# q and k transposed by DMA, the norm in four-head chunks, rsqrt by Ln and Exp: attention into a sine-gated MLP on one core

## The chip, the cores and the metric

One core of one Trainium2 chip runs the whole program. The metric is device time of one execution in microseconds (us); the kernel before has a median of 743.25 us over three runs (742.65 to 746.86).

## What is computed

Eight batches of 12 heads, 448 tokens, head size 64. q and k are normalised over the head (root mean square, with gains), then softmax attention, then an MLP over all 3584 tokens. Cut to what matters:

```python
def rmsnorm(x, g):
    rms = np.sqrt(np.mean(x * x, axis=-1, keepdims=True) + 1e-06)
    return x / rms * g
q_n, k_n = rmsnorm(q, g_q), rmsnorm(k, g_k)
attn = softmax(q_n @ k_n.T / sqrt(64))          # per batch and head
x = (attn @ v), heads side by side: 3584 x 768
h = x @ w_in                                    # 768 x 2048
g = h + sin(alpha * h)**2 / (alpha + 1e-09)
out = g @ w_out                                 # 2048 x 768
```

## The kernel before, in words

The order of the work is written out by hand; each engine takes its instructions in the order of the program, and waits where an operand is late.

**Per batch** there is an attention phase of six head pairs (index `p`), and then a first product and a second product. For a pair, `scores` (L225) makes four blocks of transposed scores on TensorE (PE) from `qkT`, ScalarE (ACT) takes the exponentials, and `attend` (L242), one pair later, multiplies by v and by a matrix of ones, which gives the row sums. ACT makes the reciprocal as Exp(-Ln(sum)) (L260, L261), and VectorE (DVE) writes the scaled result to `xT` (L264). After six pairs `first_product` (L282) runs 16 column tiles, with Sin and Square on ACT and GpSimd (POOL), and a final operation on DVE (L278). The second product of a batch (`second_product`, L312) is cut into steps of two matmuls, which are filled in between the scores of the next batch: 48 steps after an even batch, 64 after an odd one. The last batch's stand at the end.

**The norm.** q and k are loaded (L92, L98, on SP's queue) with the tokens on the partitions, in groups of six heads (`gi`, two groups per batch). `norm_tasks` (L146) gives a list of small tasks: squares on POOL (L158), sums over 64 on DVE (L161), the product of the two gains folded into k on POOL (L165), mean plus epsilon on DVE (L168), the power -0.5 on POOL for both q and k at once (L172, `inv`), and six scalings on DVE to bf16 (L178). `bg(n)` runs the next n tasks between the pieces of a pair and in the first product. At pair 2 and at the end of the batch what is left is run at once.

**The transposes.** Two pairs ahead, `transposes` (L210) turns a pair's q and k on PE into PSUM (L218, L221), and DVE copies them to `qkT` (L223). It takes one of the four PSUM bank pairs, which are handed out in a ring to scores, attend, transposes and both products.

**v** is loaded on POOL's queue, with a cast to bf16: five DMAs for each group (L92, L98). w_in comes in one DMA on POOL's queue before the first scores, w_out in one at the first pair.

Of the kernel before, what the change touches and what calls it, by code (L numbers as in the profile page):

```python
# [31 lines left out]
def kernel(  # L32
# [56 lines left out]
    def load_group(src, dst, gi, eng):  # L89
        b, h0 = gi // 2, (gi % 2) * GH  # L90
        for t in range(NT):
            eng.dma_start(  # L92
                out=dst[:, t * GH:(t + 1) * GH, :],
                in_=src[b, h0:h0 + GH, t * P:(t + 1) * P, :].rearrange("h p d -> p h d"),
            )
        rest = src[b, h0:h0 + GH, NT * P:S, :].rearrange("(pr two) p d -> two p pr d", two=2)
        for hi in range(2):
            eng.dma_start(out=dst[hi * 64:(hi + 1) * 64, NT * GH:SLOTS, :], in_=rest[hi])  # L98

    qf, kf, vb, qn, kn = {}, {}, {}, {}, {}  # L100

    def load_qk(gi):
        qf[gi] = inp.tile([P, SLOTS, D], F32, tag="qf", name="qf")
        kf[gi] = inp.tile([P, SLOTS, D], F32, tag="kf", name="kf")
        load_group(q, qf[gi], gi, nc.sync)
        load_group(k, kf[gi], gi, nc.sync)

    def load_v(gi):
        vb[gi] = vpool.tile([P, SLOTS, D], BF16, tag="vb", name="vb")
        load_group(v, vb[gi], gi, nc.gpsimd)  # L110
# [32 lines left out]
    NCH = 3  # L143
    CH = SLOTS // NCH

    def norm_tasks(gi):  # L146
# [3 lines left out]
        def begin():  # L150
            st["ms"] = npool.tile([P, 2, SLOTS], F32, tag="ms", name="ms")
            qn[gi] = npool.tile([P, SLOTS, D], BF16, tag="qn", name="qn")
            kn[gi] = npool.tile([P, SLOTS, D], BF16, tag="kn", name="kn")

        def square(which, c):
            src = (qf, kf)[which][gi]
            st[which, c] = sqpool.tile([P, CH, D], F32, tag="sq", name="sq")
            nc.gpsimd.tensor_mul(st[which, c], src[:, c * CH:(c + 1) * CH, :], src[:, c * CH:(c + 1) * CH, :])  # L158

        def reduce(which, c):  # L160
            nc.vector.reduce_sum(st["ms"][:, which, c * CH:(c + 1) * CH], st[which, c], axis=AX.X)  # L161

        def fold_g(c):
            sl = kf[gi][:, c * CH:(c + 1) * CH, :]
            nc.gpsimd.tensor_mul(sl, sl, gg.to_broadcast([P, CH, D]))  # L165

        def mean():
            nc.vector.tensor_scalar(st["ms"], st["ms"], 1.0 / D, 1e-6, op0=ALU.mult, op1=ALU.add)  # L168
# [6 lines left out]
        def scale(which, c):  # L175
            src, dst = (qf, kf)[which][gi], (qn, kn)[which][gi]
            lo = which * SLOTS + c * CH
            nc.vector.tensor_mul(  # L178
                dst[:, c * CH:(c + 1) * CH, :], src[:, c * CH:(c + 1) * CH, :],
                st["inv"][:, lo:lo + CH].unsqueeze(2).to_broadcast([P, CH, D]))  # L180

        work = [begin]
        pend = None
        for which in range(2):
            for c in range(NCH):
                work.append(lambda w=which, c=c: square(w, c))
                if pend:
                    work.append(pend)
                pend = lambda w=which, c=c: reduce(w, c)
        work.append(lambda: fold_g(0))  # L190
        work += [pend, mean, rsqrt, lambda: fold_g(1), lambda: fold_g(2)]
        for which in range(2):
            for c in range(NCH):
                work.append(lambda w=which, c=c: scale(w, c))
        return work
# [7 lines left out]
    qkT, expT, xT = {}, {}, {}  # L203

    def token_columns(b):


        return (REST, 0) if b % 2 else (0, NT * P)

    def transposes(pi):  # L210

        gi, pl = pi // GP, pi % GP
        tp = psum.tile([P, 2, 1024], BF16, tag="ps", name="tp")
# [216 lines left out]
```

## Time and profile before

| what | us |
|---|---|
| median of three runs | 743.25 |
| the profiled execution: its own time | 741.66 |
| its span | 739.9 |
| busy: PE, DVE, ACT, POOL | 542.2, 322.8, 333.8, 385.9 |

The profile is of one execution, with a span from the first to the last instruction. Durations are read from that execution, so a sum of changes stands against 741.66 us; the median is 1.6 us more. Busy shares are means over phases with different limits: PE is busy for 73% of the span, and yet there are stretches in which it waits. The TensorE clock that was granted has a mean of 0.908 of full speed.

### The profile page before, as it was taken

How to read it: one execution, taken by the hardware profiler on the slowest of the kernel's cores; microseconds unless marked ns; L12 is line 12 of the kernel's file. 1: busy time of each engine (PE TensorE's matmuls, PEld its weight loads, DVE VectorE, ACT ScalarE, POOL GpSimd, SP SyncE). 2: the span in 40 equal slices, each digit the busy share in tenths (PEclk: the TensorE clock that was granted, in tenths of full speed). 3: DMA queues.
4: the chain of work that ended last, by engine and by line, in shares of the span. 5: the costliest groups of instructions: out<-in, count | busy, mean ns of one | idle time of the engine just before them, and what ended most of it. 6: DMA issues, size and time to landing. Idle time of an engine off the chain costs nothing.

```text
span 739.9 us, 8666 instructions
## 1 busy us (share of the span) xinstructions
PE 542.2 (73%) x3296; PEld 237.9 (32%) x3296; DVE 322.8 (44%) x464; ACT 333.8 (45%) x496; POOL 385.9 (52%) x312
## 2 busy tenths in 40 slices
PE   0316567949689497859779497885779778799787
PEld 0102223414334143323234243332334323344344
DVE  2345743454434654454534635347434355321331
ACT  0114435625465245634455335652546334566530
POOL 5997943496254853587243962566625674200210
PEclk9976879979999799988899789996989978999999
DMA  9999600540423413360420704243313430000002
GB/s 160 152 199 198 83 1 0 81 54 22 97 20 79 58 51 68 40 94 23 96 18 24 114 22 97 20 97 40 67 30 41 97 41 21 1 23 22 22 16 70
DMA packets 142201, 45.46 MB, mean 61 GB/s; under 512 B 135760, under 2 KB 137808, under 8 KB 142160
## 3 DMA queue, kind: packets, MB, share of 16 engines
q1 hardware_dynamic: 95024, 33.12, 19.9%
q0 software_dynamic: 47136, 11.80, 16.2%
q8 instruction: 25, 0.41, 0.2%
q14 instruction: 16, 0.13, 0.1%
HBM read 45.69 MB, written 11.01 MB: 77 GB/s over the span
## 4 chain that ended last, share of the span: by engine, by line
PE 40%; ACT 15%; POOL 15%; DVE 14%; issue 8%; SPq 5%; DMA 2%; DVEq 0%; ACTq 0%; POOLq 0%
PE ops L324 13%; PE hps L289 13%; POOL inv L172 12%; ACT s L270 10%; PE av L258 7%; DVE kn L178 5%; ACT s L275 4%; DVE qn L178 4%; SPq L92 3%; PE sc L234 2%; POOL sq L158 2%; PE tp L218 2%; SPq L98 2%; DMA kf<-in_k_dram 1%; DVE qkT L223 1%
## 5 line engine op out<-in xcount | busy, mean ns | idle before, releaser
L289 PE MATMUL hps<-xT,w_in_sb 128*128 128x448 bf16 x768 | 171.7, 373 | 65.9 <-ACT s L270 56.2
L238 ACT ACTIVATE expT<-sc 128x896 bf16<-128x896 f32 x144 | 125.7, 914 | 186.9 <-PE sc L234 186.8
L324 PE MATMUL ops<-w_out_sb,g_sb 128*128 128x384 bf16 x896 | 177.2, 331 | 0.0
L273 POOL TENSOR_TENSOR s<-s 128x448 f32<-128x448 f32 x64 | 59.6, 932 | 210.1 <-ACT s L270 188.2
L172 POOL TENSOR_TENSOR inv<-ms,mhalf 128x42 f32<-128x42 f32 x16 | 113.4, 7087 | 63.2 <-DVE ms L168 62.9
L278 DVE SCALAR_TENSOR_TENSOR g_sb<-s,inv_alpha_sb,hps 128x448 bf16<-128x448 f32 x128 | 81.4, 677 | 133.6 <-ACT s L270 133.6
L270 ACT ACTIVATE s<-hps,alpha_sb 128x448 f32<-128x448 f32 x128 | 80.3, 627 | 113.0 <-PE hps L289 111.5
L289 PEld LDWEIGHTS <-w_in_sb 128*128 128x128 bf16 x768 | 77.4, 102 | 158.3 <-issue 102.0
L324 PEld LDWEIGHTS <-g_sb 128*128 128x128 bf16 x896 | 74.5, 98 | 66.1 <-issue 28.3
L178 DVE TENSOR_TENSOR qn<-qf,inv 128x448 bf16<-128x448 f32 x48 | 57.6, 1251 | 85.1 <-POOL inv L172 85.1
L264 DVE TENSOR_TENSOR xT<-av,rec 128x448 bf16<-128x448 f32 x48 | 29.7, 619 | 105.1 <-ACT rec L261 105.1
L234 PE MATMUL sc<-qkT 64*128 64x448 bf16 x288 | 48.3, 389 | 34.8 <-DVE xT L264 27.4
L218 PE MATMUL tp<-ident,qn 128*128 128x128 bf16 x144 | 17.5, 232 | 76.1 <-DVE qn L178 43.2
L158 POOL TENSOR_TENSOR sq<-kf 128x448 f32<-128x448 f32 x48 | 43.7, 928 | 52.5 <-DVE ms L161 52.5
L258 PE MATMUL av<-expT,vb 128*64 128x448 bf16 (+1 forms) x384 | 57.3, 399 | 3.8 <-ACT expT L238 3.3
L165 POOL TENSOR_TENSOR kf<-kf,gg 128x448 f32<-128x448 f32 x48 | 59.6, 1252 | 0.0
L161 DVE TENSOR_REDUCE ms<-sq 128x7 f32<-128x448 f32 x96 | 55.1, 609 | 6.9 <-POOL sq L158 6.8
L258 PE MATMUL av<-expT,ones 128*64 128x448 bf16 (+1 forms) x384 | 54.6, 384 | 0.0
L260 ACT ACTIVATE rec<-av 128x448 f32<-128x448 f32 x48 | 26.1, 543 | 61.9 <-PE av L258 61.9
L223 DVE COPY qkT<-tp 128x896 bf16<-128x896 bf16 x48 | 29.8, 620 | 44.8 <-PE tp L221 44.7
L158 POOL TENSOR_TENSOR sq<-qf 128x448 f32<-128x448 f32 x48 | 47.8, 1037 | 0.4 <-DMA qf<-in_q_dram 0.4
L178 DVE TENSOR_TENSOR kn<-kf,inv 128x448 bf16<-128x448 f32 x48 | 47.8, 1035 | 0.0
(33 smaller groups left out, 350.9 us busy)
## 6 DMA issues: line engine op xcount, KB each, us to landing
qf<-in_q_dram SPq DMA_DIRECT2D x48, 192.0 KB, 3.9
kf<-in_k_dram SPq DMA_DIRECT2D x48, 192.0 KB, 3.8
out_dram<-osb SPq DMA_DIRECT2D x24, 384.0 KB, 2.3
vb<-in_v_dram POOLq DMA_DIRECT2D x48, 96.0 KB, 3.4
w_in_sb<-in_moe_w_in_dram POOLq DMA_DIRECT2D x1, 3072.0 KB, 20.8
w_out_sb<-in_moe_w_out_dram POOLq DMA_DIRECT2D x1, 3072.0 KB, 22.9
qf<-in_q_dram SPq DMA_DIRECT2D x32, 48.0 KB, 3.5
kf<-in_k_dram SPq DMA_DIRECT2D x32, 48.0 KB, 3.4
```

Source lines behind the costliest of these rows:

```text
L158: nc.gpsimd.tensor_mul(st[which, c], src[:, c * CH:(c + 1) * CH, :], src[:, c * CH:(c + 1) * CH, :])
L165: nc.gpsimd.tensor_mul(sl, sl, gg.to_broadcast([P, CH, D]))
L172: nc.gpsimd.tensor_tensor(st["inv"], st["ms"].rearrange("p a s -> p (a s)"), mhalf.to_broadcast([P, 2 * SLOTS]), op=ALU.pow)
L178: nc.vector.tensor_mul(dst[:, c * CH:(c + 1) * CH, :], src[:, c * CH:(c + 1) * CH, :], st["inv"][:, lo:lo + CH].unsqueeze(2).to_broadcast( ...
L234: nc.tensor.matmul(sc[:, hi, :S], kt[r, m0 + t * P:m0 + (t + 1) * P], qt[r, :], start=True, stop=True)
L238: nc.scalar.activation(expT[pi][:, 2 * t:2 * t + 2, :], sc[:, :, :S], ACT.Exp, scale=SCALE)
L258: nc.tensor.matmul(av[r, bank, :S], lhsT, rhs, start=(t == 0), stop=(t == NT))
L270: nc.scalar.activation(s1, hps, ACT.Sin, scale=alpha_sb[:, m, :])
L273: nc.gpsimd.tensor_mul(s2, s1, s1)
L278: nc.vector.scalar_tensor_tensor(g_sb[:, m, (b % 2) * S:(b % 2 + 1) * S], s2, inv_alpha_sb[:, m, :], hps, op0=ALU.mult, op1=ALU.add)
L289: nc.tensor.matmul(ps[:, m % 2, :S], w_in_sb[:, kt, m * P:(m + 1) * P], x[:, kt, :], start=(kt == 0), stop=(kt == KT - 1))
L324: nc.tensor.matmul(st["ps"][:, half, :HALF], lhsT, w_out_sb[:, m, half * HALF:(half + 1) * HALF], start=(m == 0), stop=(m == MT - 1))
```

## The change

q and k are loaded with seven consecutive tokens of one head on a partition (448 = 64 x 7), and two heads on the two halves of the partitions, so that a chunk (`ci`, three per batch) is four heads of q and of k in one tile, loaded by two DMAs. A chunk's norm has eight tasks. POOL squares 896 columns at a time and folds the gains; DVE takes the sums; ACT makes Ln (with the mean's factor and epsilon) and Exp(-0.5 x); DVE scales to bf16 in four operations of 448 columns. Then two DMA transposes on SP's queue write `qkT` for the chunk's two pairs, with no PE, no PSUM and no copy on DVE. `qkT` has nine buffers in place of four. The tasks of the next batch's three chunks, each with its load ahead, are run during this batch's attention phase, one for each of 24 slots (two in batch 0, which makes its own chunks 1 and 2 as well), what is left at the phase's end, and none in the first product. v comes in twelve DMAs per batch, issued on POOL at the start of the phase. The rows of w_in are permuted, and it is loaded in 16 DMAs during pairs 0 to 3 of batch 0; w_out follows at pair 4. The outputs go to interleaved rows, two DMAs for each 128 rows.

```diff
-    vpool = ctx.enter_context(tc.tile_pool(name="vpool", bufs=4))
+    vpool = ctx.enter_context(tc.tile_pool(name="vpool", bufs=2))
-    tpool = ctx.enter_context(tc.tile_pool(name="qkT", bufs=4))
+    tpool = ctx.enter_context(tc.tile_pool(name="qkT", bufs=9))
...
+    def load_qk(ci):
+        b, dp = ci // NC, ci % NC
+        qk[ci] = inp.tile([P, 2, 2 * NJ, D], F32, tag="qk", name="qk")
+        for which, src in ((0, q), (1, k)):
+            heads = src[b, 4 * dp:4 * dp + 4].rearrange("(hi pp) (p j) d -> (pp p) hi (j d)", pp=2, j=NJ)
+            nc.sync.dma_start(out=qk[ci][:, which].rearrange("p (hi j) d -> p hi (j d)", hi=2), in_=heads)
+    def load_v(b):
+        vb[b] = vpool.tile([P, NT * H + NP, D], BF16, tag="vb", name="vb")
+        tok = v[b].rearrange("h (p j) d -> j p h d", j=NJ)
         for t in range(NT):
+            for jj in range(2):
+                nc.gpsimd.dma_start(out=vb[b][jj * 64:jj * 64 + 64, t * H:(t + 1) * H, :], in_=tok[2 * t + jj])
...
         def rsqrt():
-            st["inv"] = npool.tile([P, 2 * SLOTS], F32, tag="inv", name="inv")
-            nc.gpsimd.tensor_tensor(
-                st["inv"], st["ms"].rearrange("p a s -> p (a s)"), mhalf.to_broadcast([P, 2 * SLOTS]), op=ALU.pow)
+            st["inv"] = npool.tile([P, 2, 2 * NJ], F32, tag="inv", name="inv")
+            nc.scalar.activation(st["inv"], st["ms"], ACT.Ln, scale=1.0 / D, bias=eps)
+            nc.scalar.activation(st["inv"], st["inv"], ACT.Exp, scale=-0.5)
...
+        def transpose():
+            for pp in range(2):
+                pi = 2 * ci + pp
+                qkT[pi] = tpool.tile([P, 2, S], BF16, tag="qkT", name="qkT")
+                nc.sync.dma_start_transpose(
+                    out=qkT[pi].rearrange("p w (j t) -> p (w j) t", t=REST),
+                    in_=st["n"][pp * 64:pp * 64 + 64].rearrange("p w j hi d -> p (w j hi d)"))
+        return [lambda: square(0), lambda: square(1), lambda: (reduce(0), fold_g()), lambda: reduce(1), rsqrt,
+                lambda: scale(0), lambda: scale(1), transpose]
...
-        nc.vector.tensor_copy(qkT[pi], tp[:, 0, :2 * S].rearrange("p (a s) -> p a s", a=2))
...
+        per_slot = 1 if b else 2
         if b + 1 < B:
-            load_qk(2 * b + 2)
-            load_v(2 * b + 2)
+            for ci in range(NC * (b + 1), NC * (b + 2)):
+                background.append(lambda ci=ci: load_qk(ci))
+                background.extend(norm_tasks(ci))
+            if b:
+                load_v(b + 1)
```

How the queues change, at three places. **SP, in the attention phase of a batch with 48 filled steps** (DMA issues; `qkT<-qkn` is a DMA transpose, `osb` a result on its way out). Before:

```order
L332 DMA out_dram<-osb 128x768
L92 DMA qf<-in_q_dram 128x6x64 x3
L98 DMA qf<-in_q_dram 64x3x64 x2
L92 DMA kf<-in_k_dram 128x6x64 x3
L98 DMA kf<-in_k_dram 64x3x64 x2
L332 DMA out_dram<-osb 128x768 x2
```

and changed:

```order
L96 DMA qk<-in_q_dram 128x2x448
L96 DMA qk<-in_k_dram 128x2x448
L306 DMA out_dram<-osb 64x768 x2
L185 DMA_TRANSPOSE qkT<-qkn 128x14x64 x2
L96 DMA qk<-in_q_dram 128x2x448
L96 DMA qk<-in_k_dram 128x2x448
```

The load of a chunk now stands behind the transposes of the chunk before it, which wait for that chunk's scaling.

**POOL, from the start of an attention phase**, before:

```order
L92 DMA vb<-in_v_dram 128x6x64 x3
L98 DMA vb<-in_v_dram 64x3x64 x2
L158 TENSOR_TENSOR sq<-qf 128x448 x3
L158 TENSOR_TENSOR sq<-kf 128x448 x3
L165 TENSOR_TENSOR kf<-kf,gg 128x448
L172 TENSOR_TENSOR inv<-ms,mhalf 128x42
L165 TENSOR_TENSOR kf<-kf,gg 128x448 x2
```

and changed:

```order
L105 DMA vb<-in_v_dram 64x12x64 x6
L109 DMA vb<-in_v_dram 64x2x64 x6
L159 TENSOR_TENSOR sq<-qk 128x896 x2
L162 TENSOR_TENSOR qk<-qk,gg 128x896
L159 TENSOR_TENSOR sq<-qk 128x896 x2
L162 TENSOR_TENSOR qk<-qk,gg 128x896
```

The power is gone from POOL, and all of the next batch's v stands ahead of the first square.

**ACT, from the start of an attention phase** (`expT` the exponentials, `rec` the reciprocal of a row sum), before:

```order
L355 ACT_TABLE_LOAD
L238 ACTIVATE expT<-sc 128x896 x3
L240 ACTIVATE expT<-sc 128x448
L238 ACTIVATE expT<-sc 128x896 x2
L260 ACTIVATE rec<-av 128x448
L261 ACTIVATE rec<-rec 128x448
L238 ACTIVATE expT<-sc 128x896
```

and changed:

```order
L326 ACT_TABLE_LOAD
L210 ACTIVATE expT<-sc 128x896 x3
L212 ACTIVATE expT<-sc 128x448
L210 ACTIVATE expT<-sc 128x896 x2
L232 ACTIVATE rec<-av 128x448
L233 ACTIVATE rec<-rec 128x448
L169 ACTIVATE inv<-ms,eps 128x28
L170 ACTIVATE inv<-inv 128x28
L210 ACTIVATE expT<-sc 128x896
```

Three times in a phase the two small operations of a chunk stand among the exponentials, and the exponentials behind them wait when the chunk's sums are late.

## Rows read from the trace of the kernel before

**Rows 1.** Windows: start:end, length, busy (x instructions), clock granted, DMA share, GB/s.

```profile
0.00:129.53 129.53, 59.77 (x328) 24.04 (x329) 58.69 (x85) 41.38 (x62) 93.30 (x78) 0.84 0.73 113
129.53:299.80 170.27, 132.12 (x824) 58.11 (x824) 80.08 (x116) 83.42 (x125) 95.61 (x77) 0.93 0.34 57
...
647.57:739.90 92.33, 78.58 (x496) 37.79 (x495) 23.87 (x35) 41.64 (x62) 7.46 (x8) 0.99 0.08 30
```

**Rows 2.** Chain that ended last, in order of time, 385 to 475 us.

```profile
407.56 7.10 POOL inv L172
...
418.23 4.21 DVE kn L178 x3
...
434.18 7.10 POOL inv L172
...
447.86 0.55 DVE xT L264
...
472.74 1.28 ACT L355
```

**Rows 3.** Timeline of the last batch: start, duration, engine, line, operation.

```profile
666.06 0.55 PE L234 MATMUL sc<-qkT 64*128 64x448 bf16 x4
...
672.89 0.55 PE L234 MATMUL sc<-qkT 64*128 64x448 bf16 x4
...
678.89 0.55 PE L234 MATMUL sc<-qkT 64*128 64x448 bf16 x4
...
688.17 0.62 DVE L264 TENSOR_TENSOR xT<-av,rec 128x448 bf16<-128x448 f32 x1 [2.22 <-ACT rec L261]
...
713.44 20.96 PE L324 MATMUL ops<-w_out_sb,g_sb 128*128 128x384 bf16 x128
```

**Rows 4.** Groups by line and shape: busy us, mean ns of one, idle before.

```profile
L165 POOL TENSOR_TENSOR kf<-kf,gg 128x448 f32<-128x448 f32 x48 | 59.6, 1252 | 0.0
...
L161 DVE TENSOR_REDUCE ms<-sq 128x7 f32<-128x448 f32 x96 | 55.1, 609 | 6.9 <-POOL sq L158 6.8
...
L158 POOL TENSOR_TENSOR sq<-kf 128x448 f32<-128x448 f32 x48 | 43.7, 928 | 52.5 <-DVE ms L161 52.5
L92 POOL DMA_DIRECT2D vb<-in_v_dram x48 | 41.4, 874 | 0.1
...
L260 ACT ACTIVATE rec<-av 128x448 f32<-128x448 f32 x48 | 26.1, 543 | 61.9 <-PE av L258 61.9
...
L98 POOL DMA_DIRECT2D vb<-in_v_dram x32 | 20.4, 660 | 0.4 <-DMA qf<-in_q_dram 0.4
```

**Rows 5.** Timeline at single places of DVE, POOL, ACT, PE and SP's queue.

```profile
15.03 1.78 SPq L92 DMA_DIRECT2D kf<-in_k_dram  x3
...
29.70 1.68 DVE L178 TENSOR_TENSOR kn<-kf,inv 128x448 bf16<-128x448 f32 x3
...
32.88 1.30 PE L234 MATMUL sc<-qkT 64*128 64x448 bf16 x6
...
357.78 0.61 DVE L264 TENSOR_TENSOR xT<-av,rec 128x448 bf16<-128x448 f32 x1
...
383.86 2.60 POOL L92 DMA_DIRECT2D vb<-in_v_dram  x3
...
385.56 1.28 ACT L355 ACT_TABLE_LOAD   x1
...
414.68 3.55 DVE L178 TENSOR_TENSOR qn<-qf,inv 128x448 bf16<-128x448 f32 x3 [7.20 <-POOL inv L172]
```

**Rows 6.** DMA: a queue (packets, MB, share), then issues (KB each, us to landing).

```profile
q0 software_dynamic: 47136, 11.80, 16.2%
...
qf<-in_q_dram SPq DMA_DIRECT2D x48, 192.0 KB, 3.9
...
w_out_sb<-in_moe_w_out_dram POOLq DMA_DIRECT2D x1, 3072.0 KB, 22.9
```

**Rows 7.** Windows as in rows 1: a stretch with the DMA engines full.

```profile
33.00:60.00 27.00, 8.75 (x54) 3.06 (x54) 13.52 (x16) 7.05 (x10) 25.28 (x20) 0.71 1.27 198
```

More of the change, by code (lines that the diff above doesn't have):

```diff
@@ L87, in bank_pair @@
         return psum.tile([P, 2, 512], F32, tag="ps", name=name)
-    def load_group(src, dst, gi, eng):
-        b, h0 = gi // 2, (gi % 2) * GH
-        for t in range(NT):
[L92 to L96, printed above, removed]
-        for hi in range(2):
[L98 to L110, printed above, removed]
+    qk, vb = {}, {}
+    def load_qk(ci):
[7 more added lines that the diff above has]
+        tok = v[b].rearrange("h (p j) d -> j p h d", j=NJ)
+        for t in range(NT):
+            for jj in range(2):
+                nc.gpsimd.dma_start(out=vb[b][jj * 64:jj * 64 + 64, t * H:(t + 1) * H, :], in_=tok[2 * t + jj])
+        last = v[b].rearrange("(dp hi pp) (p j) d -> j hi p dp pp d", hi=2, pp=2, j=NJ)[NJ - 1]
+        for hi in range(2):
+            for dp in range(NC):
+                nc.gpsimd.dma_start(
+                    out=vb[b][hi * 64:hi * 64 + 64, NT * H + 2 * dp:NT * H + 2 * dp + 2, :], in_=last[hi, :, dp])
     load_qk(0)
@@ L133, with load_alpha, load_w_in @@
     inv_alpha_sb = wpool.tile([P, MT, 1], F32)
-    def load_weights():
+    def load_alpha():
         nc.sync.dma_start(out=alpha_sb, in_=moe_alpha.rearrange("(mt p a) -> p mt a", p=P, a=1))
         nc.vector.reciprocal(inv_alpha_sb, alpha_sb)
-        nc.gpsimd.dma_start(out=w_in_sb, in_=moe_w_in.rearrange("(kt p) f -> p kt f", p=P))
+    WCH = 4
+    def load_w_in(c):
+        cols = slice(c * (D_FF // WCH), (c + 1) * (D_FF // WCH))
+        rows = moe_w_in[:, cols].rearrange("(dp hi pp d) f -> hi pp d dp f", dp=NC, hi=2, pp=2)
+        dst = w_in_sb[:, :, cols].rearrange("p (dp pp) f -> p pp dp f", pp=2)
+        for hi in range(2):
+            for pp in range(2):
+                nc.gpsimd.dma_start(out=dst[hi * 64:hi * 64 + 64, pp], in_=rows[hi, pp])
@@ L140, in load_w_out, with norm_tasks @@
     def load_w_out():
         nc.gpsimd.dma_start(out=w_out_sb, in_=moe_w_out.rearrange("(mt p) d -> p mt d", p=P))
-    NCH = 3
-    CH = SLOTS // NCH
-    def norm_tasks(gi):
+    qkT, expT, xT = {}, {}, {}
+    def norm_tasks(ci):
         st = {}
[L150 to L168, printed above, removed]
-        def rsqrt():
-            st["inv"] = npool.tile([P, 2 * SLOTS], F32, tag="inv", name="inv")
-            nc.gpsimd.tensor_tensor(
-                st["inv"], st["ms"].rearrange("p a s -> p (a s)"), mhalf.to_broadcast([P, 2 * SLOTS]), op=ALU.pow)
[L175 to L195, printed above, removed]
@@ L201, in bg @@
             background.popleft()()
[L203 to L213, printed above, removed]
-        for which, src in ((0, qn[gi]), (1, kn[gi])):
-            o = tp[:, 0, which * S:(which + 1) * S]
-            m0, r0 = token_columns(pi // NP)
-            for t in range(NT):
-                nc.tensor.transpose(o[:, m0 + t * P:m0 + (t + 1) * P], src[:, t * GH + 2 * pl:t * GH + 2 * pl + 2, :], ident)
-            for hi in range(2):
-                r = slice(hi * 64, hi * 64 + 64)
-                nc.tensor.transpose(o[r, r0:r0 + REST], src[r, NT * GH + pl, :], ident[r, r])
-        qkT[pi] = tpool.tile([P, 2, S], BF16, tag="qkT", name="qkT")
-        nc.vector.tensor_copy(qkT[pi], tp[:, 0, :2 * S].rearrange("p (a s) -> p a s", a=2))
     def scores(pi, t):
@@ L233, in scores @@
             if t < NT:
[L234 removed]
+                nc.tensor.matmul(sc[:, hi, :S], kt[r, t * P:(t + 1) * P], qt[r, :], start=True, stop=True)
             else:
[L236 removed]
+                nc.tensor.matmul(sc[r, 0, :S], kt[r, NT * P:S], qt[r, :], start=True, stop=True)
         if t < NT:
@@ L314, in second_product @@
         steps = []
-        for i in range(NT + b % 2):
+        odd = b % 2
+        rows = [out[c * S:(c + 1) * S, :].rearrange("(p j) d -> j p d", j=NJ) for c in range(B)]
+        for i in range(NT + odd):
             st = {}
```

108 lines of the change are left out of this document (53 added, 55 removed).

## The prediction

> **What bounds the kernel now.** I read the busy time by batch first, then the chain of waits, then the timeline. From 129.53 to 647.57 us run six batches that each carry the norm of the next: 518.0 us, 86.3 each. The last batch carries none and takes 92.3 us with its whole second product and the last output at the end. In a pair of the normed batches PE is busy for 132 of 170 us, in the last batch, with its unpaired first product, for 79 of 92; no engine is full in the normed ones (POOL 96 of 170 us) [rows 1]. So it is a latency: the chain of one batch goes through the power on POOL twice, 7.10 us each, then through the scalings that wait for it, and the first product begins only behind the last of them [rows 2]. The second product's filling of PE does not help, because the transposes, and with them all later scores, stand behind those scalings.
>
> The phase without a norm gives PE's own pace. In the last batch a pair with transposes takes 6.83 us (666.06 to 672.89), one without 6.00 (672.89 to 678.89): transposes cost 0.83 us a pair. From the load of the exponentials' table (647.57) to the last `xT` (688.17 + 0.62) it takes 41.2 us with four pairs of transposes; without them 37.9. A batch with 64 filled steps in place of 48 has 32 more matmuls of 0.164 us (20.96 by 128), so 43.1 [rows 1, 3]. From the last `xT` to the next table load, the first product takes 24.3 us (448.41 to 472.74) and 27.2 (358.39 to 385.56): 25.8 is my mean [rows 2, 5].
>
> **What the change removes.** The power on POOL, PE's transposes with DVE's copies, and the norm from the first product. A norm now has a whole batch of lead. What it adds is a second line of work beside PE, in which a chunk's load waits on SP behind the transposes of the chunk before. If three chunks take longer than PE's 37.9 or 43.1 us, they set the phase, since the last chunk's scalings stand ahead of the last `xT` on DVE.
>
> **One chunk, by rows.** Two squares of 896 columns: 2 x 2 x 0.93 = 3.7 us on POOL. The second sum: 2 x 0.61 = 1.2; the first runs beside the second square, and the folding (2 x 1.25) beside the sum and what follows [rows 4]. Ln and Exp of 28 columns are not in the trace; below is nothing, above the 0.54 that 448 columns take each [rows 4]. I take 0.7 with the handing over, between the ends since the columns shrink but the start of an instruction does not. Four scalings of 448 columns: 0.56 each while POOL is quiet (1.68 by 3), 1.18 beside POOL's work (3.55 by 3) [rows 5]; that is 2.2 to 4.7, and I take 3.0, since the folding covers the first or second alone. Sum: 8.6 us.
>
> **Between chunks.** The step from the last scaling to the next square is the disputed price; I call it X. Two transposes of 64 x 1792 values in bf16 move 229 KB each. The nearest row is the loads of q and k in runs of 256 bytes, which 128 bf16 columns also are: with the engines full they ran at 198 GB/s [rows 7], so 1.16 us each, 2.3 for both. The load of q is 459 KB; w_out came at 6.29 MB in 22.9 us, or 275 GB/s, which gives 1.7. A load of 197 KB lands after 3.9 us, of which 1.0 is transfer, so 2.9 is fixed [rows 6]. X = 2.3 + 1.7 + 2.9 = 6.9, say 7. The lower end is 5.8: the transposes cost no more than two issues of 0.59 (1.78 by 3) on SP [rows 5]. The upper end is a rival's.
>
> [...]
>
> **A changed batch.** Count from the table load. POOL starts on v before it (383.86 against 385.56, so at -1.7) [rows 5], and now issues all twelve DMAs first: 6 x 0.87 + 6 x 0.66 = 9.2 us [rows 4], to 7.5. The first chunk was loaded during the first product: 8.6 us, to 16.1. The second: 7 + 8.6, to 31.7. The third: 47.3. The last `xT`: 47.9. That is over PE's 43.1 and 37.9, so the chunks set both kinds of batch. With the first product 73.7 us, against 86.3. Six batches: 518 - 442 = **76 us less**. The two outputs for one and the strided rows lie beside this on SP (0.6 us more per 128 rows), ahead of transposes that are not due yet; they cost nothing while the chunks are as late as that. Behind a waiting transpose on SP stand the next load, which is in X, and outputs, of which three can be in hand before PE would feel it.
>
> **The first stage** ends at 129.5 us now [rows 1]. POOL issues twelve DMAs, of which the last four wait for the first to land, amid 2.75 MB of q and k; the squares start at 10.6 at the earliest, at 18 if v is slow. I take 14. Then 8.6 to 22.6, and the first transpose lands 4.5 later (the 3.9 of a load and an issue): scores at 27, against 32.9 [rows 5, 6]. Chunk 1's Ln stands on ACT behind three exponentials of pair 0 (to 31), chunk 2's behind those of pair 1 (41). Both were loaded early. Chunks 3 to 5, for batch 1, each wait for their load: 15.6 us each, so 56, 72 and 88, and ACT holds the remaining pairs between. Pair 5's exponentials and reciprocals take 8 more, to 96, and the first product 25, near the mean above: 121. **8.5 us less**. w_out, issued at about 98 behind v, lands at 98 + 22.9 = 121, just when the filling wants it; its cover is gone if v is slower.
>
> **The last batch** loses four pairs of transposes: **3.3 us less**. Sum: 76 + 8.5 + 3.3 = 88, from 741.7 to 654 us of the profiled execution; against the median, which is 1.6 higher, **655**. X stands twice in each of six batches and three times in the first stage, so a microsecond of X is 15 us, and X = 7 + 88/15 = 12.9 gives all back.
>
> **Rivals.**
> 1. *The transposes are slow on the DMA queue: slower than now.* They write 1792 runs of 128 bytes each. The queue that casts v also writes runs of 128 bytes: 47,136 packets in 16.2% of 16 engines' 739.9 us are 40.7 ns each [rows 6]. At that price a transpose takes 1792 x 40.7 ns / 16 = 4.6 us, both 9.1, X grows by 6.8, and the time is 655 + 102 = 757. It decides from 4.1 us per transpose on. For it speaks the size of the runs; against it, that v's packets also pay for a cast. Chance 0.13.
> 2. *SP is held while it issues a transpose.* Each microsecond of holding counts twice in X, 30 us of time. An issue of 768 runs takes 0.59 us [rows 5]; in proportion to 1792 runs it is 1.4, which would give 680, inside my range. From 3 us more per transpose the change loses. Chance that it is that long: 0.04. [...]
> 3. *The waits stretch PE's own line.* While DVE waits for a late square, `xT` behind it is late; while ACT waits for a sum, the exponentials are; and the PSUM ring stops PE, whose clock is then lower (0.71 in the stretch of rows 7, 0.99 in the last batch of rows 1). Three such waits of 4 to 5 us on top of 43.1 make a phase of about 56, 8 us over mine: 655 + 48 = 703. Chance 0.17.
> 4. *All at the lower ends.* X 5.8, scalings 2.2, Ln and Exp 0.3: 6 us less in a phase, 41.9, so that PE's 43.1 sets half of the batches; with a first product of 24.3, six batches give 41 more, the first stage 7: about 607. Chance 0.2.
>
> **How the numbers follow.** My forecast (630 to 680) has 0.40, rivals 4, 3, 1 and 2 have 0.2, 0.17, 0.13 and 0.04; 0.03 is between 703 and 739, and 0.03 no change. The range is 605 to 738: it takes in rivals 3 and 4 and X up to 12.5, and leaves out rivals 1 and 2 and no change, with what may lie under 605, some 0.2. A change of less than 0.5% can't be told from none here. Faster by more: 0.40 + 0.20 + 0.17 + 0.03 = 0.80; within it 0.03; slower 0.17.
>
> **What would show it.** In the changed profile: table loads 73 to 75 us apart in the middle; a DMA transpose landing within some 4 us of its issue, at most 1.4 us of SP's queue each; POOL's first square of a phase 9 us behind the start of its v issues; its second pair of squares waiting for the load of q for 3 to 6 us; the last `xT` right behind scalings; first scores at 25 to 31 us. I am wrong if the transposes take over 4 us of the queue each, if phases are over 53 us with short X (rival 3), or if they are as short as PE's own (the chunks are then not the line that sets the end).

## The result, and the profile after

The changed kernel takes 693.37 us (median of four, 687.49 to 698.13) against 742.95 for the one before (740.75 to 746.86): a ratio of 0.930, 95% interval 0.922 to 0.938. It is faster, and the time lies in the range, but 38 us over the 655 forecast: some 50 us came where 88 were written down. Ratios here leave out disturbed executions (one of run 4 took 2512.99 us, its cause open), so they can stand a little beside the medians; gains below are ratios times 743 us (the change: 52 us), good to some 8 us when two are compared.

The profiled execution took 694.43 us, with a span of 692.6 in place of 739.9. The windows of the changed kernel, cut at the loads of the exponentials' table (columns as in [rows 1]):

```profile
0.00:141.67 141.67, 53.34 (x249) 19.11 (x250) 48.88 (x61) 43.77 (x75) 70.61 (x74) 0.87 0.76 120
141.67:213.63 71.96, 61.77 (x338) 24.15 (x337) 29.64 (x44) 42.48 (x68) 31.71 (x30) 0.93 0.48 84
213.63:292.19 78.56, 66.21 (x369) 26.99 (x370) 30.36 (x45) 43.19 (x69) 31.72 (x30) 0.93 0.45 82
292.19:363.57 71.38, 59.29 (x338) 23.80 (x337) 29.45 (x44) 42.37 (x69) 31.72 (x30) 0.98 0.47 85
363.57:446.73 83.16, 70.38 (x369) 28.08 (x370) 30.34 (x45) 43.42 (x69) 31.71 (x30) 0.88 0.43 78
446.73:519.95 73.22, 60.20 (x338) 23.93 (x337) 29.44 (x44) 42.38 (x69) 31.70 (x30) 0.95 0.46 83
519.95:600.12 80.17, 67.91 (x369) 27.39 (x370) 30.34 (x45) 43.29 (x68) 30.08 (x27) 0.91 0.40 69
600.12:692.60 92.48, 79.66 (x457) 35.75 (x455) 21.39 (x31) 41.19 (x62) 7.46 (x8) 0.95 0.12 31
```

Against [rows 1] the first stage is 12.1 us longer (129.53 to 141.67), where 8.5 less was forecast. The six normed batches take 458.45 us: 59.6 less than 518.0, where 76 less was forecast. The last batch stays as it was (92.33 to 92.48), where 3.3 less was forecast. The batches come in two kinds: about 72 us with 48 filled steps, near the 73.7 of the forecast, and 79 to 83 with 64.

**Where the first stage loses.** Single places of its timeline, POOL, DVE, SP's queue and ACT (start, duration, engine, line, operation; in brackets the idle time before and what ended it):

```profile
12.26 0.59 POOL L109 DMA_DIRECT2D vb<-in_v_dram  x1 [5.14 <-DMA vb<-in_v_dram]
...
20.34 3.32 POOL L159 TENSOR_TENSOR sq<-qk 128x896 f32<-128x896 f32 x2
...
25.43 7.31 DVE L177 TENSOR_TENSOR qkn<-qk,inv 128x448 bf16<-128x448 f32 x4 [0.64 <-ACT inv L170]
...
32.77 3.47 SPq L185 DMA_TRANSPOSE qkT<-qkn  x2
...
40.09 2.54 ACT L210 ACTIVATE expT<-sc 128x896 bf16<-128x896 f32 x3 [14.70 <-PE sc L206]
...
42.76 0.26 DVE L133 RECIPROCAL inv_alpha_sb<-alpha_sb 128x16 f32<-128x16 f32 x1 [10.01 <-DMA alpha_sb<-in_moe_alpha_dram]
44.97 0.32 ACT L169 ACTIVATE inv<-ms,eps 128x28 f32<-128x28 f32 x1 [2.34 <-DVE ms L165]
...
104.99 0.32 ACT L169 ACTIVATE inv<-ms,eps 128x28 f32<-128x28 f32 x1 [12.43 <-DVE ms L165]
```

POOL's later issues of v wait for earlier ones to land (the last four for 10.8 us in all), so the first squares start at 20.3 us. The scalings that follow take 7.31 us for four, beside POOL's next squares and folding. The first transposes are issued at 32.8, and the first exponentials run at 40.1. A second wait stands beside this: alpha's load is issued on SP behind those transposes (at 36.3), and DVE waits 10.0 us for it, with chunk 1's sums behind it, so that ACT, free at 42.6, makes chunk 1's Ln only at 45.0. Chunk 5's Ln stands at 105.0.

**Where a batch with 64 steps loses.** The first such batch by the windows above (213.63 to 292.19), SP's queue first, then POOL, then DVE:

```profile
228.11 3.01 SPq L185 DMA_TRANSPOSE qkT<-qkn  x2
231.23 0.90 SPq L96 DMA_DIRECT2D qk<-in_q_dram  x1
...
236.38 13.88 SPq L306 DMA_DIRECT2D out_dram<-osb  x4
250.36 3.24 SPq L185 DMA_TRANSPOSE qkT<-qkn  x2
253.69 0.98 SPq L96 DMA_DIRECT2D qk<-in_q_dram  x1
...
211.94 4.53 POOL L105 DMA_DIRECT2D vb<-in_v_dram  x6
...
220.00 3.37 POOL L159 TENSOR_TENSOR sq<-qk 128x896 f32<-128x896 f32 x2
...
235.68 3.32 POOL L159 TENSOR_TENSOR sq<-qk 128x896 f32<-128x896 f32 x2 [10.14 <-DMA qk<-in_q_dram]
...
258.14 3.32 POOL L159 TENSOR_TENSOR sq<-qk 128x896 f32<-128x896 f32 x2 [16.98 <-DMA qk<-in_q_dram]
...
225.81 2.22 DVE L177 TENSOR_TENSOR qkn<-qk,inv 128x448 bf16<-128x448 f32 x4
...
242.94 2.23 DVE L177 TENSOR_TENSOR qkn<-qk,inv 128x448 bf16<-128x448 f32 x4 [0.64 <-ACT inv L170]
...
248.19 0.95 DVE L302 COPY osb<-ops 128x768 f32<-128x768 f32 x1
```

X, the step from a chunk's last scaling to the next square, is 7.65 us the first time (225.81 + 2.22 = 228.03 to 235.68), against 7 forecast. The second time it is 13.0 (245.17 to 258.14). The scaling ended at 245.17, but on SP the chunk's transposes stand behind an output whose result DVE writes only at 248.19 to 249.14; they start at 250.36, and the load of the third chunk waits behind them.

**The terms of a chunk**, in the groups by line and shape (busy us, mean ns of one, idle before and what ended it):

```profile
L159 POOL TENSOR_TENSOR sq<-qk 128x896 f32<-128x896 f32 x48 | 81.5, 1733 | 185.7 <-DMA qk<-in_q_dram 176.3 <-DVE ms L165 9.3
L177 DVE TENSOR_TENSOR qkn<-qk,inv 128x448 bf16<-128x448 f32 x96 | 64.3, 727 | 6.1 <-ACT inv L170 5.8
...
L169 ACT ACTIVATE inv<-ms,eps 128x28 f32<-128x28 f32 x24 | 7.6, 318 | 104.1 <-DVE ms L165 104.1
L170 ACT ACTIVATE inv<-inv 128x28 f32<-128x28 f32 x24 | 5.4, 226 | 0.8
```

POOL waits 176.3 us for loads of q: the chunks' line is the serial line that the forecast took it for. The transposes in the same execution, issues (ns of SP's queue: least, median, most) and landing:

```profile
L185 SPq DMA_TRANSPOSE qkT<-qkn x48: 1230/1620/2497, 32.8 to 573.4; - x48
...
DMA to landing us min/median/max: 3.5/3.9/9.5
```

**Where the first product loses.** Windows from the last `xT` to the next table load (two with 64 steps, and between them one with 48), then three short ones around the end of the phase at 416:

```profile
266.24:292.19 25.95, 19.02 (x85) 8.24 (x85) 9.43 (x15) 14.10 (x25) 9.10 (x11) 0.87 0.24 53
338.38:363.57 25.19, 18.07 (x91) 8.31 (x90) 9.44 (x15) 13.98 (x25) 9.10 (x11) 1.00 0.25 56
416.73:446.73 30.00, 23.18 (x85) 9.31 (x85) 9.44 (x16) 14.32 (x25) 9.10 (x11) 0.72 0.21 47
...
409.00:413.00 4.00, 3.91 (x22) 1.92 (x21) 2.09 (x3) 0.00 (x0) 3.92 (x3) 1.00 0.01 2
413.00:417.00 4.00, 0.21 (x1) 0.10 (x1) 3.73 (x7) 2.83 (x5) 1.11 (x1) 0.91 0.38 98
417.00:421.00 4.00, 1.74 (x5) 0.50 (x4) 1.27 (x2) 2.37 (x4) 1.42 (x2) 0.50 0.81 116
```

With the clock at 1.00 the first product takes 25.2 us. After PE stood nearly still from 413 to 417, waiting for the late last `xT`, its granted clock was 0.50, and this product took 30.0.

### The profile page after: what moved, and what is told of

It is laid out like the page before. It is cut to its first block, busy times and chain, and to the rows that moved or that the text cites. A ratio compares the mean times of both kernels' runs of the same rounds, so it can differ in the third digit from the quotient of the medians.

```text
span 692.6 us, 7553 instructions
## 1 busy us (share of the span) xinstructions
PE 518.8 (75%) x2816; PEld 209.2 (30%) x2816; DVE 249.8 (36%) x352; ACT 342.1 (49%) x544; POOL 266.7 (39%) x253
## 3 DMA queue, kind: packets, MB, share of 16 engines
q1 hardware_dynamic: 64432, 44.13, 27.6%
## 4 chain that ended last, share of the span: by engine, by line
PE 45%; ACT 16%; POOL 14%; DMA 9%; DVE 7%; issue 5%; SPq 3%; DVEq 0%; ACTq 0%; POOLq 0%
PE hps L261 16%; PE ops L298 16%; ACT s L242 10%; PE av L230 9%; POOL sq L159 6%; DMA qk<-in_q_dram 6%; POOL vb L105 4%; ACT s L247 4%; PE sc L206 3%; POOL vb L109 3%; DVE qkn L177 3%; SPq L185 3%; DMA vb<-in_v_dram 2%; DVE ms L165 2%; PE sc L208 1%
## 5 line engine op out<-in xcount | busy, mean ns | idle before, releaser
L298 PE MATMUL ops<-w_out_sb,g_sb 128*128 128x384 bf16 x896 | 186.7, 336 | 1.6 <-ACT expT L210 1.6
L159 POOL TENSOR_TENSOR sq<-qk 128x896 f32<-128x896 f32 x48 | 81.5, 1733 | 185.7 <-DMA qk<-in_q_dram 176.3
L298 PEld LDWEIGHTS <-g_sb 128*128 128x128 bf16 x896 | 72.4, 99 | 77.4 <-issue 46.6
L165 DVE TENSOR_REDUCE ms<-sq 128x14 f32<-128x896 f32 x48 | 51.6, 1082 | 116.7 <-POOL sq L159 116.6
L177 DVE TENSOR_TENSOR qkn<-qk,inv 128x448 bf16<-128x448 f32 x96 | 64.3, 727 | 6.1 <-ACT inv L170 5.8
L169 ACT ACTIVATE inv<-ms,eps 128x28 f32<-128x28 f32 x24 | 7.6, 318 | 104.1 <-DVE ms L165 104.1
L162 POOL TENSOR_TENSOR qk<-qk,gg 128x896 f32<-128x896 f32 x24 | 50.4, 2100 | 1.9
L206 PEld LDWEIGHTS <-qkT 64*128 64x128 bf16 x288 | 15.0, 94 | 112.4 <-issue 59.6
L208 PE MATMUL sc<-qkT 64*64 64x448 bf16 x96 | 19.3, 395 | 28.5 <-ACT expT L210 22.1
L247 ACT ACTIVATE s<-s 128x448 f32<-128x448 f32 x64 | 36.9, 576 | 2.0
L105 POOL DMA_DIRECT2D vb<-in_v_dram x48 | 36.4, 788 | 0.8 <-POOLq L378 0.8
```

Source lines behind the costliest of these rows:

```text
L105: nc.gpsimd.dma_start(out=vb[b][jj * 64:jj * 64 + 64, t * H:(t + 1) * H, :], in_=tok[2 * t + jj])
L159: nc.gpsimd.tensor_mul(st[w], qk[ci][:, w], qk[ci][:, w])
L165: nc.vector.reduce_sum(st["ms"][:, w, :], st[w], axis=AX.X)
L177: nc.vector.tensor_mul(st["n"][:, w, :, hi, :], qk[ci][:, w, js], st["inv"][:, w, js].unsqueeze(2).to_broadcast([P, NJ, D]))
L206: nc.tensor.matmul(sc[:, hi, :S], kt[r, t * P:(t + 1) * P], qt[r, :], start=True, stop=True)
L247: nc.scalar.activation(s2, s1, ACT.Square)
```

## The experiments

**1. The power alone.** The kernel before, with only the power replaced (and, not in the lines below, the first load of the exponentials' table moved ahead of the first norm, so that Ln and Exp have it in time):

```diff
-            nc.gpsimd.tensor_tensor(
-                st["inv"], st["ms"].rearrange("p a s -> p (a s)"), mhalf.to_broadcast([P, 2 * SLOTS]), op=ALU.pow)
+            nc.scalar.activation(st["inv"], st["ms"].rearrange("p a s -> p (a s)"), ACT.Ln)
+            nc.scalar.activation(st["inv"], st["inv"], ACT.Exp, scale=-0.5)
```

> The kernel before with one part of the change alone: the power on POOL (7.1 us) becomes Ln and Exp on ACT (0.6 us), nothing else. Theory (latency of the norm's chain sets the normed batches): two powers per batch lie in the chain, so about 14 x 6.5 = 91 us go where each is wholly on the path, and 40 to 90 us if some is covered: 655 to 705 us against 743. Rival (the gain came from the DMA transposes and the batch of lead, the power was covered by other work): less than 20 us, 725 to 743.

Measured: 652.38 us, ratio 0.876 (0.870 to 0.882), a gain of 92 us, just beyond the forecast. That is more than the whole change gives. Windows by table loads: the first stage, the six batches together, and the longest of them:

```profile
0.00:114.99 114.99, 62.02 (x328) 24.78 (x329) 56.48 (x85) 42.64 (x70) 62.74 (x74) 0.81 0.82 128
114.99:557.40 442.41, 383.30 (x2472) 171.62 (x2472) 214.09 (x346) 254.04 (x397) 195.31 (x215) 0.99 0.38 63
...
482.55:557.40 74.85, 65.98 (x428) 30.13 (x428) 35.17 (x59) 42.17 (x67) 30.75 (x35) 1.00 0.30 50
```

The batches take 71.7 to 74.9 us, 11.4 to 14.6 under the mean of 86.3, about the two powers of [rows 2] (14.2) less what replaces them, and the first stage 14.5 less. Not all of it is the wait itself: for the same 2472 matmuls in these six batches PE is busy 383.3 us, where it was 403.8 before, at a granted clock of 0.99 in place of 0.91. So the other parts of the change together gave back about 40 us.

**2. The load ahead.** A chunk's load is issued two chunks earlier, ahead of the norm of the chunk that is two before it (the lines below are for the batches; the first stage has the same):

```diff
-                background.append(lambda ci=ci: load_qk(ci))
+                if ci + 2 < B * NC:
+                    background.append(lambda ci=ci: load_qk(ci + 2))
```

> The changed kernel with each chunk's load issued two chunks earlier, in the same three buffers and at the same place in SP's queue, so that no load stands between two chunks. Theory (the chunks' line of transposes, load, squares sets the phases): X of 7.5 us in even and 13 us in odd batches leaves twice a phase, phases fall to PE's own 38 and 43 us plus some 2, so 5 us less in even and 7 in odd batches, and 3 x 7 in the first stage: 640 to 665 against 693. Rival (in-order waits of ACT and DVE and the clock set the phases, not the loads): under 10 us.

Measured: 656.41 us, ratio 0.881 (0.875 to 0.888), 36 us better than the change, and inside the forecast. POOL's timeline has the second chunk's squares right behind the first chunk's folding, with no wait for a load:

```profile
207.50 2.08 POOL L162 TENSOR_TENSOR qk<-qk,gg 128x896 f32<-128x896 f32 x1
209.54 3.70 POOL L159 TENSOR_TENSOR sq<-qk 128x896 f32<-128x896 f32 x2
```

The load that stands behind the waiting transposes is thus what makes X serial. But the gain is not where the forecast had it. In the profiled execution the first stage is 15.7 us shorter (125.95), and the batches with 64 steps fall to between 74.7 and 75.1, 17.1 us in all; those with 48 steps stay at 71.5 to 71.9, 1.6 us less for all three, where 5 us less was expected of each. A phase of such a batch, in a window from table load to table load:

```profile
125.95:168.17 42.22, 38.07 (x240) 14.37 (x239) 24.73 (x27) 27.11 (x44) 23.92 (x19) 1.00 0.62 101
```

It is 2.2 us shorter than in the change (141.67 to 186.05), with PE now busy for 38.07 of 42.22 us, and DVE for 24.73 (18.22 in the change); what the phase won, the first product took back (29.4 us from 168.17 on, for 27.6; the granted clock is 1.00 in the phase and 0.95 over the whole batch). So X held the first stage and the batches with 64 steps; with 48 steps it was on the path, and little is won by taking it alone out. That the total met the forecast is luck in part.

**3. The outputs behind.** The output DMAs are held back to the end of each pair:

```diff
-                        nc.sync.dma_start(out=dst, in_=o[jj * 64:jj * 64 + 64, :])
+                        held.append(lambda dst=dst, src=o[jj * 64:jj * 64 + 64, :]: nc.sync.dma_start(out=dst, in_=src))
...
+            if p < NP - 1:
+                release()
```

> The changed kernel with each result's two output DMAs issued at the end of its pair, so behind that pair's transposes and loads on SP's queue. Theory (in the batches with 64 filled steps the second chunk's transposes and the third's load stand on SP behind outputs that wait for their result, 5 us of 13): the batches of 78 to 83 us fall by about 5 us each, those of 72 us stay, 693 to about 678. Rival (SP's order is no term): within 3 us of 693.

Measured: 674.59 us, ratio 0.905 (0.897 to 0.913), 19 us better than the change. The three batches with 64 steps fell from 78.6, 83.2 and 80.2 to 74.6, 74.75 and 76.1; the first stage stayed (142.4). Of those with 48, one rose from 71.4 to 76.6, 29.4 of it the first product, for 25.2 in the change; the other two stayed. On SP's queue the transposes now go ahead of the outputs:

```profile
245.99 3.01 SPq L185 DMA_TRANSPOSE qkT<-qkn  x2
...
250.65 1.13 SPq L306 DMA_DIRECT2D out_dram<-osb  x2
```

**4. The first stage.** On POOL v of batch 0 goes behind chunk 0's squares and folding; alpha's load goes ahead of chunks 1 and 2:

```diff
+    nc.sync.dma_start(out=alpha_sb, in_=moe_alpha.rearrange("(mt p a) -> p mt a", p=P, a=1))
     load_qk(1)
     load_qk(2)
...
-    load_v(0)
     background.extend(norm_tasks(0))
     bg(len(background))
+    load_v(0)
```

> The changed kernel with the first batch's v issued behind the first chunk's norm on POOL, and alpha's load ahead of chunks 1 and 2 on SP. Theory (the last four v DMAs wait for the first, so the first squares start at 20.3 us, and beside them the scalings are slow): first squares at 7 to 9, first exponentials at 27 to 30 in place of 40, the first stage 10 us shorter or somewhat less: 680 to 687. Rival (the first stage is set by chunks 3 to 5 and their loads alone, which take up what is won): within 4 us of 693.

Measured: 672.53 us, ratio 0.902 (0.894 to 0.910), 21 us better than the change, more than either theory had. POOL and ACT:

```profile
4.20 3.32 POOL L159 TENSOR_TENSOR sq<-qk 128x896 f32<-128x896 f32 x2 [3.75 <-DMA qk<-in_q_dram]
...
20.45 2.54 ACT L210 ACTIVATE expT<-sc 128x896 bf16<-128x896 f32 x3 [10.25 <-PE sc L206]
```

The squares start 16 us earlier and the first exponentials 20 (20.45 for 40.09). The stage ends at 124.5, 17.2 earlier, where some 10 was expected. Two things moved at once: DVE no longer waits for alpha either. The squares are v's part; what of the 17.2 us is alpha's was not tried by itself.

**5. v later.** The twelve issues of the next batch's v go behind pair 1, for every batch from the second on:

```diff
-            if b:
-                load_v(b + 1)
...
+            if b and p == 1 and b + 1 < B:
+                load_v(b + 1)
```

> The changed kernel with the twelve v DMAs of the next batch issued after pair 1 of a phase, while POOL waits for the second chunk's load, and not at the phase's start. Theory (the 8 us of issues stand ahead of the first square and shift the whole line of chunks): phases 5 to 8 us shorter in batches 1 to 6 as far as PE's own 38 and 43 us allow: 653 to 670. Rival (later waits take it up): within 5 us of 693.

Measured: 671.38 us, ratio 0.894 (0.885 to 0.903), 27 us better than the change. Its batches are 67.4 to 68.7 us with 48 steps and 74.6 to 75.3 with 64. In the batch whose table load is at 207.85, POOL's first squares start at 206.17, 1.7 us ahead of it; in the change they start 6.4 us behind it (220.00 against 213.63). So the 8.1 us that POOL spends on v ahead of the first square (211.94 to 220.00) were on the path in each batch, as the forecast had them, and cost 3 to 8 us of each.

**6. Each transpose twice**, the second into a tile that nobody reads:

```diff
+                nc.sync.dma_start_transpose(
+                    out=scratch.rearrange("p w (j t) -> p (w j) t", t=REST),
+                    in_=st["n"][pp * 64:pp * 64 + 64].rearrange("p w j hi d -> p (w j hi d)"))
```

> The changed kernel with each DMA transpose issued a second time, to a tile that nobody reads: the disputed price doubled. Theory (two transposes hold SP's queue for 3.3 us between the last scaling and the next load, twice in each of six batches and three times in the first stage): 15 x 3.3 = 50 us more, about 740. Rival (a transpose costs nothing on the path since its queue has room): within 5 us of 693. If a transpose takes the DMA engines longer than SP: over 760.

Measured: 757.05 us, ratio 1.018 (1.011 to 1.025), 65 us worse than the change, 17 over the theory's 740. SP's queue at one chunk:

```profile
281.59 1.31 SPq L186 DMA_TRANSPOSE qkT<-qkn  x1
282.94 1.92 SPq L189 DMA_TRANSPOSE scratch<-qkn  x1
...
287.39 1.23 SPq L189 DMA_TRANSPOSE scratch<-qkn  x1
288.71 0.98 SPq L96 DMA_DIRECT2D qk<-in_q_dram  x1
```

The two more issues hold SP for 3.15 us, and the six batches are 40.4 us longer (498.9 for 458.45), 3.4 for each of twelve X. So in the batches a transpose is paid, nearly all of it, as time of SP's queue. The first stage grew by 21 us, 7 for each X, where the theory had 3.3; why is open, and with it most of the 17 us. All the added transposes write one tile, so some may have waited for one another; that was not separated.

**7. The transposes back on PE**, 14 per pair into PSUM and a copy on DVE, at the same place of the program:

```diff
-                nc.sync.dma_start_transpose(
...
+                        nc.tensor.transpose(
+                            tp[:, 0, c:c + REST], st["n"][r, w, j].rearrange("p hi d -> p (hi d)"), ident[r, r])
...
+                nc.vector.tensor_copy(qkT[pi], tp[:, 0, :2 * S].rearrange("p (a s) -> p a s", a=2))
```

> The changed kernel with the DMA transposes undone: 14 transposes of 64 columns per pair on PE into PSUM and a copy on DVE, at the same place in the program. Theory (the DMA transposes win by taking PE out of the wait for the scalings): PE now waits at each chunk for scalings that are late, and does 48 x 1.3 us more; X is 3.3 us shorter; on balance 10 to 60 us slower: 703 to 755. Rival (the 3.3 us on SP cost more than PE would): faster, 650 to 690.

Measured: 732.12 us, ratio 0.982 (0.977 to 0.988), 39 us worse than the change. In the waits of PE's queue, `PE tp L191 <- DVE qkn L179` has 89.0 us in 26 waits. Most of it lies in the first stage, which is 9.7 us shorter all the same (131.99); 25.6 us in 15 waits lie in the six batches, which are 46.6 us longer together. There PE's later work stands behind a late scaling. Runs 10 and 11 separate that wait from the transposes' own time.

**8. The power again**, in the changed kernel, with the mean back on DVE:

```diff
-            nc.scalar.activation(st["inv"], st["ms"], ACT.Ln, scale=1.0 / D, bias=eps)
-            nc.scalar.activation(st["inv"], st["inv"], ACT.Exp, scale=-0.5)
+            nc.vector.tensor_scalar(st["ms"], st["ms"], 1.0 / D, 1e-6, op0=ALU.mult, op1=ALU.add)
+            nc.gpsimd.tensor_tensor(
...
+                mhalf.to_broadcast([P, 4 * NJ]), op=ALU.pow)
```

> The changed kernel with the power on POOL again (28 columns for q and k, about 4.7 us by the columns, or 7.1 if its time does not depend on them), with mean and epsilon on DVE. Theory (a chunk's own latency is in the line three times a phase): three times 4.5 to 6.5 us in each of six batches, and five or six in the first stage: 90 to 150 us slower, 785 to 845. Rival (a batch of lead hides it): within 15 us of 693.

Measured: 801.45 us, ratio 1.076 (1.070 to 1.083), 109 us worse than the change. Its group:

```profile
L172 POOL TENSOR_TENSOR inv<-ms,mhalf 128x28 f32<-128x28 f32 x24 | 115.1, 4796 | 14.9 <-DVE ms L171 12.8
```

The batches grew by 81.5 us, 4.5 in the mean for each of 18 chunks: the power's 4.80 less 0.54 for Ln and Exp, and the mean's operation on DVE. So a chunk's own time counts three times in a batch, as the forecast had it; by batch it is 14.1 to 18.6 us with 48 steps, and 8.7 to 13.1 with 64, where some of it is covered.

**9. Edits 2 to 5 together.**

> The changed kernel with the four edits of E2 to E5 together: loads two chunks ahead, outputs behind the transposes, v after pair 1, and v of batch 0 and alpha moved in the first stage. Theory (the four remove waits of one line of chunks, and PE's own pace is the next limit): even batches near 67, odd near 72 to 75, the first stage near 110, so 620 to 640; less than the sum of the four gains (37 + 19 + 21 + 22 = 99, which would be 594), since PE's floor holds. Rival (they are independent): 594 to 610.

Measured: 621.88 us, ratio 0.829 (0.822 to 0.836): the fastest of all, 75 us better than the change. Windows: the first stage, and two batches, each cut at the load of the table for Sin, so into its phase and the rest:

```profile
0.00:100.28 100.28, 52.36 (x249) 18.58 (x250) 56.12 (x61) 43.67 (x75) 71.37 (x73) 0.88 1.19 188
100.28:139.00 38.72, 37.84 (x240) 14.09 (x239) 22.50 (x27) 27.09 (x43) 23.32 (x20) 1.00 0.68 110
139.00:168.64 29.64, 22.63 (x100) 9.95 (x98) 11.05 (x19) 15.48 (x26) 9.11 (x10) 0.88 0.26 60
168.64:213.13 44.49, 43.05 (x271) 17.24 (x272) 28.21 (x29) 27.81 (x43) 23.70 (x20) 1.00 0.64 105
213.13:239.95 26.82, 19.70 (x100) 9.14 (x98) 10.41 (x17) 15.27 (x26) 9.11 (x10) 1.00 0.27 66
```

The two batches take 68.4 and 71.3 us, the other four 68.4 to 71.3. Alone the four edits gave 36, 19, 21 and 27, together 75 and not 103: each shortens the same line, and once it is short, PE's own pace sets the phase, with PE busy for 37.84 of 38.72 and for 43.05 of 44.49 us. By the prediction's own numbers a batch at that pace is 63.7 (37.9 + 25.8) and 68.9 us.

**10. Run 9 with PE's transposes** at the place of the DMA's (the edit of run 7).

> E9 with the DMA transposes undone, as in E7 (14 transposes a pair on PE and a copy on DVE). Theory (once nothing is late, a DMA transpose is worth PE's time and a little waiting): 48 pairs x 1.3 us = 62 us of PE at the most, and 12 to 20 us of waits, so 670 to 710 against E9. Rival (PE has idle time for it): within 15 us of E9.

Measured: 727.17 us, ratio 0.977 (0.970 to 0.983), 110 us worse than run 9, which no theory had. PE waits 104.8 us in 41 waits for scalings, 56.4 of it in the six batches, and phases are 54.8 to 60.5 us. With the loads two chunks ahead, PE still comes to the transposes before the scalings are there. So run 7 did not price the transposes.

**11. Run 9 with PE's transposes two pairs ahead of use**, as the kernel before has them, out of a tile kept for longer:

```diff
+                if pi + 2 < B * NP:
+                    transposes(pi + 2)
```

> E9 with the transposes on PE again, but two pairs ahead of their use, as in the kernel before, and not right behind the scalings. In E10 PE waited for the scalings at each chunk. Theory (E10's 105 us over E9 are mostly PE standing behind late scalings; a DMA transpose itself is worth PE's time): 28 transposes of a chunk took 1.4 to 1.6 us of PE in E10, so 0.75 us a pair and 36 us for 48 pairs, with the copy's wait for PSUM some more: 650 to 670. Rival (transposes on PE cost what E10 shows wherever they stand): over 700. If PE has room for them: within 10 us of E9's 622.

Measured: 651.80 us, ratio 0.878 (0.874 to 0.883), 37 us worse than run 9. PE is busy with 48 pairs of transposes for 30.5 us in all, 0.64 a pair (the 1.3 of runs 7 and 10 was an estimate, which no run shows), and DVE with their copies for 29.6. So in this order of the work 37 us is what the DMA transposes are worth, most of it PE's own time. Run 11 is level with run 1: its first stage is 6.5 us shorter (108.47 for 114.99) and its six batches 3.7 longer (446.08 for 442.41). Beside the power and the DMA transposes, all the rest of the change, the norm in chunks a batch ahead with it and with the edits of runs 2 to 5, gives nothing together that can be told.

## Why the prediction was right, and where it was wrong

**The account.** From 743: the power is worth 92 us (run 1), the DMA transposes 37 (run 11 against 9), and four places in the order of the queues give back 75 (run 9). 92 + 37 - 75 = 54, and 52 were measured. What closes this account is that run 11, reached from the changed kernel, comes out level with run 1, reached from the one before; once they are level the sum holds by itself. Of the 75, half lies in the first stage: 41.4 us of 81.1 between the two profiled executions (100.28 for 141.67). The miss against the 654 forecast for the profiled execution is 40 us: 16.3 in the six batches, 20.6 in the first stage, 3.4 in the last batch.

**Right.** The latency through the power bounded the kernel (run 1). The changed batch is set by a serial line of chunks and X: lengthening a chunk or X lengthens every kind of batch (runs 8, 6), and an earlier start shortens them (run 5). Taking X out by itself shortened only those with 64 steps; with 48 the phase won 2.2 us and the first product lost 1.8 (run 2). X is 7.65 us where nothing stands in the way, for 7 forecast: but it is 3.0 of SP's queue for two transposes (228.11 to 231.12) and 4.45 from the load's issue to the square (231.23 to 235.68), where I had 2.3 for the transposes' transfer and 4.6 for the load. Scalings of a chunk: 2.7 us (64.3 by 24) for 3.0. Ln and Exp: 0.32 and 0.23, so 0.54, for 0.7. The 48-step batches have their last `xT` 46.2 to 48.0 us after the table load, for 47.9, and 25.2 to 25.6 of first product, for 25.8. One sign did not follow from the working: the second squares were to wait 3 to 6 us for q, but a step of 15.6 us less 6.2 of POOL's own work is 9.4, and 10.1 was measured.

**Luck.** The time lies in the range because the range was wide. Its upper part was made for a longer X and for PE's line stretched by waits; what filled it is, for half, a first stage that the forecast had moving the other way.

**Wrong: "they cost nothing while the chunks are as late as that" (outputs on SP).** In the 64-step batches the last `xT` stands 52.6, 53.2 and 52.5 us after the table load, not 47.9: 14.6 us over three batches. The prediction argued that outputs stand ahead of transposes that are not due yet, and looked only at what outputs behind a waiting transpose do. The other order was the one that mattered: a transpose, and with it the next load, behind an output that waits for PE. Run 3 took it away, and those batches got shorter by 16.4 us in all.

**Wrong: the first stage, 8.5 us less.** It was 20.6 us off. Squares at 20.3, not 14, are 6.3 of it, beyond the upper end of 18 that I had named. The first scalings ended at 32.7, not 22.6: 3.8 more, since 4.7 was my upper end for the scalings and they took 7.3 beside POOL's squares and folding. The first exponentials came at 40.1, 7.3 after the transposes' issue, where I had scores 4.5 behind it: 2 to 3 more. Alpha's load stood in no term; chunk 1's Ln waits 2.3 us for the sums behind it and comes at 45.0, for 31. Chunks 3 to 5 then follow one another by 16.2, 18.2 and 16.9 us, for 15.6, so that at chunk 5's Ln the miss was 17 (105.0 for 88), and the rest came in what follows. Run 4, which moves v and alpha, takes 17.2 us out of the stage; its squares start 16 us earlier, so v's place is probably the larger part, but the two were not tried apart.

**Mis-sized: the first product, 25.8 us.** In the 64-step batches it was 25.95, 30.0 and 27.65, 6.2 us more in all. The last `xT` is late there, PE idles before it, and the granted clock is 0.87, 0.72 and 0.81 in what follows. Lateness is not all of it: in run 3, where the last `xT` is back at 46.1 to 47.6, these products still take 27.1 to 28.7. The other small differences in the six batches come to 4.5 us the other way; 14.6 + 6.2 - 4.5 is the 16.3 missed there.

**Mis-sized: the last batch, 3.3 us less.** The attention phase did lose 2.4 us (600.12 to 638.30 is 38.2, before it was 40.6). The products behind it took 54.3 us in place of 51.75, with a granted clock of 0.91 for 0.98, and gave it back. In run 9, at 0.99, the last batch takes 89.84, near the 89.0 of the forecast.

**The rivals.** The first (4.6 us a transpose on the DMA queue) is out: they land after 3.9 us, as a plain load does [rows 6], and doubling them cost SP's time. The second was real but small: 1.62 us of SP's queue each in the median and 2.50 at the most, near the 1.4 worked out in proportion to the runs. Its 680 counted only what 1.4 is above a plain issue of 0.59; the whole of it, beside the 2.3 of transfer, would have made 697. In what was measured the holding stands in place of the transfer. The third gave 703, near the measured time, by a mechanism that runs 2 to 5 put elsewhere: the waits stretched the chunks' line on SP and POOL, and PE only after it. The fourth (PE's pace sets half of the batches, 607) is near what run 9 made of the kernel, but by taking X out of the line, not by X at its lower end.

**Left open.** Run 9's batches are 2 to 7 us over PE's own pace. The phases shown are at that pace, so the rest lies behind them: the last `xT` comes 40.3 and 45.5 us after the table load, for 37.9 and 43.1, and what follows the phase takes 29.6 us in two of the three batches with 48 steps, at a granted clock of 0.88 in the one shown, and 26.8 in the third (over a whole batch the clock is 0.95 in all three, and 1.00 in those with 64). What lowers the clock there was not tried. Its scalings took 1.26 us in the mean, for 0.73 in the change. Of PE's waits for DMA transposes, 33.1 us in three, the longest 20.7, none is in a batch: all are in the first stage.

## What to carry to other kernels

Before a large rebuild, take the one slow operation on the chain and replace it alone: here that gave more than the rebuild (92 us for 52). On a queue that takes its work in order, a load must not stand behind something that waits for the result of the piece before (36 us here, run 2), and one lists for each queue what stands ahead of an item that is due as well as what stands behind it. A move of work to PE's own queue is priced only where its inputs are ready (two pairs ahead here); right behind a late producer the same instructions cost 110 us in place of 37.

## What was not expected of the hardware

- A DMA transpose of 64 x 1792 bf16 values holds SP's queue for 1.23 to 2.50 us in the changed kernel (median 1.62; 6.23 at the most in run 9), where the load of a chunk's q or k (448 KB) takes 0.95 (q) and 0.47 (k) in the median and 4.8 at the most; it lands after 3.9 us in the median, and 9.5 at the most, in the first stage.
- Scalings of 448 columns on DVE took 0.56 us while POOL was quiet (2.23 by 4) and 1.83 beside POOL's squares and folding of 896 (7.31 by 4), over three times as long.
- The power on POOL took 0.17 us a column in both sizes: 7.10 us for 42 [rows 2], 4.80 for 28 (run 8). On ACT Ln and Exp took 0.24 us each for 42 columns (run 1).
- After a wait of 3.9 us PE's granted clock went from 1.00 to 0.50 and stayed there in the next windows (417 to 430 us); it was back at 1.00 from 435, and the first product was 4.8 us longer (30.0 for 25.2). That a wait of this length is what it takes is not shown: in the same execution the first products of two batches with 48 steps begin with waits of 0.72 and 1.73 us, and the granted clock fell to 0.50 in the one (191.4 to 194.3) and stayed at 1.00 in the other (340.3 to 346.2).
